# Ln and Exp ahead of the Relu check in every chunk of a gated linear attention, with a tile of its own for the Relu

## The chip, the cores and the metric

The kernel runs on one core of one Trainium2 chip. The metric is the device time of one execution in microseconds (us). A core has TensorE (PE, matrix products), VectorE (DVE), ScalarE (ACT, activation functions), GpSimd (POOL) and SyncE (SP, which issues the DMAs here). Each engine works through its own queue of instructions in order and waits at semaphores for the others. The program groups the functions of ScalarE into sets of tables, and an instruction ACT_TABLE_LOAD changes the set.

## The reference

A gated linear attention over 4 batches, 8 heads, 768 steps and a head size of 48 runs first, then a feed-forward block on its output (3072 tokens, width 384, inner width 2048):

```python
for t in range(S):
    state = alpha[:, :, t, :, None] * state + np.einsum('bhd,bhe->bhde', k[:, :, t], v[:, :, t])
    y[:, :, t] = np.einsum('bhd,bhde->bhe', q[:, :, t], state)
...
h = x @ w_in
sp = np.maximum(h, 0.0) + np.log1p(np.exp(-np.abs(h)))
g = h * erf(sp)
return (g @ w_out).astype(np.float32)
```

All tensors are float32.

## The kernel before

The attention is cut into 24 chunks of 64 steps (two groups of batches, 12 chunks each), each chunk holding 4 pairs of heads and 2 batches side by side as tiles of 128 x 512. The feed-forward block is cut into 12 blocks of 256 tokens, and each block into 4 groups of 512 inner channels. A feed-forward block starts when its two chunks of attention are done, so both parts run interleaved over the whole time.

In a chunk (class `Chunk`) the steps are: `la`, `lq`, `lv` load alpha, k with q, and v. `a1` (L260) makes the cumulative products of alpha in place in the tile A, on VectorE, with a floor. `a2` (L263 to L280) makes the reciprocal of A: on ScalarE a Relu with bias -AHI over A (L266), whose sum goes into `flags` and tells whether any product went above AHI; then Ln of A (L267), then Exp of its negative (L269), whose sum goes into `flags` too, and on VectorE one Newton step (`rw`, L273 and L275) and the product with k (L278). `a3` (L283) multiplies q by A. `a4` makes the scores (`pS`, L298), the update of the state T (`pu`, L307, with `kn`, the transposed k that ScalarE copies), and the masked scores `sT`. `a5` makes the attention's output `py` and splits it into a rounded part `x_hi` (L220, a copy) and the rest `x_lo` (L395, VectorE).

In a feed-forward block (class `Moe`) H is the first product (`ph`, L429, and its copy `hs`), U a Tanh on ScalarE, L1 two Ln and one Exp, L2 two VectorE passes (L458, L460), G a Gelu, Z two VectorE passes (L469, L471), O the second product (`acc`, L495) on a rounded half `gh` and a rest `gl` (L484, VectorE), and `out` the store. Steps `wi` and `wo` load the weights and split them (tiles `wst`, `wbuf`, `wi_hi`, `wo_hi` and so on).

Ln and Exp are in one set of ScalarE's tables (`LNEXP` in the code), Tanh and Gelu in another (`GELU`). The helper `act` (L210 to L214) remembers the set that it loaded last and puts an ACT_TABLE_LOAD (L213) ahead of a function of the other. Relu and Copy don't go through it:

```python
def act(table, *args, **kw):
    if loaded[0] != table:
        loaded[0] = table
        nc.scalar.preload_act_table_set(table)
    nc.scalar.activation(*args, **kw)
```

The order of all work is written out by hand in a string SCHED: each word is one step of a generator, and a generator's `yield` ends a step. So the words of `a2` take one piece of that function after another: the first word the Relu, the second the Ln, the third the Exp, and the next three one VectorE pass each. Words of other steps stand between them. Around chunk 7 and chunk 18 SCHED reads:

```
... v:H_2_0_0 a2_7 G_0_3 U_1_1 wo_13 a2_7 a2_7 a2_7 ...
... U_7_2 a5_16 H_7_3_1 a2_18 a2_17 U_6_3 H_7_3_1 a4_16 ... a2_18 a2_18 ...
```

The tile `r` comes from a pool with one buffer for each name, so the r of one chunk is the r of the next. `general` is a slow way for inputs whose flags are raised; it is compiled in but doesn't run here.

Of the kernel before, what the change touches and what calls it, by code (L numbers as in the profile page):

```python
# [10 lines left out]
F32 = mybir.dt.float32  # L11
# [5 lines left out]
AF = mybir.ActivationFunctionType  # L17
# [4 lines left out]
AHI = 1e15  # L22
# [125 lines left out]
def gla_moe(ctx: ExitStack, tc: tile.TileContext, qk, v, alpha, w_in, w_out, out):  # L148
    nc = tc.nc


    M, CPB, P, _, NP, NI, TC = qk.shape
# [17 lines left out]
    at = fast.enter_context(tc.tile_pool(name="at", bufs=1))  # L170
# [20 lines left out]
    flags = const.tile([P, NS, 2], F32, name="flags")  # L191
# [18 lines left out]
# [5 lines that stand above are left out]
# [9 lines left out]
            nc.vector.tensor_scalar(out=out, in0=in_, scalar1=scale, scalar2=None, op0=ALU.mult)  # L224

    T = at.tile([P, NI * NP * HD], F32, name="T", tag="T")
    nc.gpsimd.memset(T, 0.0)
    Tv = T.rearrange("p (i a d) -> p i a d", i=NI, a=NP)[:, :, :, :D]

# [3 lines left out]
    class Chunk:  # L233
# [29 lines left out]
        def a2(self):  # L263
            A = self.A[:, :, 1:]
            r = at.tile([P, NP * NI, TC], F32, name="r", tag="r")
            nc.scalar.activation(r, A, AF.Relu, bias=-AHI, accum_out=flags[:, self.n, 1:2])  # L266
            yield  # L267
            act(LNEXP, r, A, AF.Ln)
            yield  # L269
            act(LNEXP, r, r, AF.Exp, scale=-1.0, accum_out=flags[:, self.n, 0:1])  # L270
            yield
            w = at.tile([P, NP * NI, TC], F32, name="rw", tag="rw")
            nc.vector.tensor_tensor(out=w, in0=A, in1=r, op=ALU.mult)  # L273
            yield
            nc.vector.scalar_tensor_tensor(out=w, in0=w, scalar=2.0, in1=r, op0=ALU.subtract, op1=ALU.mult)  # L275
            yield
            kk = self.kq[:, 0].rearrange("p a i t -> p (a i) t")
            nc.vector.tensor_tensor(out=kk, in0=kk, in1=w, op=ALU.mult)  # L278
            yield
# [64 lines left out]
        def a5(self):  # L344
# [6 lines left out]
            for kt in range(KT):  # L351
                sums = []
                for w, d0 in PIECES[kt]:
                    if not self.first:
                        sums.append((w, d0, T, D, self.Q))
                    sums.append((w, d0, vx, HD, self.sT))
# [393 lines left out]
```

## Time and profile before

| what | value |
| --- | --- |
| median of 3 runs | 528.25 us (526.23 to 528.33) |
| the profiled execution | 526.75 us |
| its span in the profile | 525.0 us |
| PE busy | 499.5 us (95%) |
| DVE busy | 497.3 us (95%) |
| ACT busy | 485.1 us (92%) |
| table loads | 53 |
| granted TensorE clock, mean | 0.997 |

The span is what the profiler sees of the engines; the execution's own time is 1.75 us longer. A busy engine is one that works on an instruction. Matmuls are pipelined and their ends are modelled, so TensorE's busy time says little about its pace. Times of instructions are microseconds from the start of the span. An accumulated sum shows as a small instruction of its own, ACTIVATION_READ_ACCUMULATOR, right behind its activation. In a group the last columns are the engine's idle time directly ahead of its instructions and what ended it.

### The profile page before, as it was taken

How to read it: one execution, taken by the hardware profiler on the slowest of the kernel's cores; microseconds unless marked ns; L12 is line 12 of the kernel's file. 1: busy time of each engine (PE TensorE's matmuls, PEld its weight loads, DVE VectorE, ACT ScalarE, POOL GpSimd, SP SyncE). 2: the span in 40 equal slices, each digit the busy share in tenths (PEclk: the TensorE clock that was granted, in tenths of full speed). 3: DMA queues.
4: the chain of work that ended last, by engine and by line, in shares of the span. 5: the costliest groups of instructions: out<-in, count | busy, mean ns of one | idle time of the engine just before them, and what ended most of it. 6: DMA issues, size and time to landing. Idle time of an engine off the chain costs nothing.

```text
span 525.0 us, 16780 instructions
## 1 busy us (share of the span) xinstructions
PE 499.5 (95%) x7386; PEld 481.5 (92%) x7386; DVE 497.3 (95%) x715; ACT 485.1 (92%) x700; POOL 2.3 (0%) x14
## 2 busy tenths in 40 slices
PE   1699999999999999999999999999999999999994
PEld 1599999989999999999999999999999999999994
DVE  6999999999999999999999999999899999999993
ACT  6999999999999999989999899998898999999680
POOL 1000000000000000000000000000000000000000
PEclk9999999999999999999999999999999999999998
DMA  8976353341313203413012311123103120000001
GB/s 296 346 284 237 105 161 114 125 151 41 127 37 93 90 30 107 156 55 134 2 58 67 117 37 38 59 72 109 44 23 121 43 79 26 8 1 30 28 4 37
DMA packets 17936, 48.44 MB, mean 92 GB/s; under 512 B 1984, under 2 KB 5056, under 8 KB 17856
## 3 DMA queue, kind: packets, MB, share of 16 engines
q1 hardware_dynamic: 17856, 47.29, 26.6%
q8 instruction: 60, 0.98, 0.8%
q14 instruction: 20, 0.16, 0.1%
HBM read 42.57 MB, written 4.72 MB: 90 GB/s over the span
## 4 chain that ended last, share of the span: by engine, by line
PE 48%; ACT 25%; DVE 18%; issue 4%; DMA 3%; SPq 0%; DVEq 0%; ACTq 0%
PE acc L495 25%; PE ph L429 18%; ACT s L214 6%; ACT w L214 3%; ACT L213 3%; PE py L364 3%; ACT hs L220 3%; DVE t L458 2%; DVE gl L484 2%; ACT r L214 2%; DVE w L460 2%; DMA A<-in_alpha_dram 2%; ACT wbuf L220 2%; ACT wbuf L532 2%; DVE s L469 2%
## 5 line engine op out<-in xcount | busy, mean ns | idle before, releaser
L429 PE MATMUL ph<-x_hi,wi_hi 128*128 128x256 f32 x576 | 165.8, 288 | 1.8 <-ACT x_hi L220 1.1
L429 PE MATMUL ph<-x_lo,wi_hi 128*128 128x256 f32 x576 | 161.6, 281 | 1.1 <-issue 0.9
L429 PE MATMUL ph<-x_hi,wi_lo 128*128 128x256 f32 x576 | 161.3, 280 | 0.2 <-issue 0.2
L495 PE MATMUL acc<-wo_hi,gh 128*128 128x384 f32 x384 | 130.9, 341 | 0.0
L495 PE MATMUL acc<-wo_hi,gl 128*128 128x384 f32 x384 | 129.9, 338 | 0.8 <-DVE gl L484 0.6
L495 PE MATMUL acc<-wo_lo,gh 128*128 128x384 f32 x384 | 129.1, 336 | 0.0
L429 PEld LDWEIGHTS ph<-x_hi,wi_hi 128*128 128x128 f32 x576 | 109.0, 189 | 5.4 <-ACT hs L220 1.9
L429 PEld LDWEIGHTS ph<-x_hi,wi_lo 128*128 128x128 f32 x576 | 109.8, 191 | 1.0 <-issue 1.0
L429 PEld LDWEIGHTS ph<-x_lo,wi_hi 128*128 128x128 f32 x576 | 109.1, 189 | 0.6 <-DVE x_lo L395 0.5
L214 ACT ACTIVATE s<-s 128x1024 f32<-128x1024 f32 x96 | 100.1, 1054 | 6.2 <-DVE t L458 5.9
L495 PEld LDWEIGHTS acc<-wo_hi,gl 128*128 128x128 f32 x384 | 72.2, 188 | 2.6 <-DVE gl L484 2.4
L495 PEld LDWEIGHTS acc<-wo_hi,gh 128*128 128x128 f32 x384 | 72.2, 188 | 1.2
L495 PEld LDWEIGHTS acc<-wo_lo,gh 128*128 128x128 f32 x384 | 72.2, 188 | 0.0
L484 DVE TENSOR_TENSOR gl<-hs,gh 128x512 fp32r<-128x512 f32 x96 | 65.0, 689 | 6.5 <-ACT gh L220 1.7
L213 ACT ACT_TABLE_LOAD x52 | 66.7, 1283 | 0.9
L471 DVE SCALAR_TENSOR_TENSOR hs<-s,hs 128x1024 f32<-128x1024 f32 x48 | 58.6, 1222 | 0.7
L458 DVE TENSOR_TENSOR t<-s,w 128x1024 f32<-128x1024 f32 x48 | 58.2, 1219 | 1.0 <-ACT w L214 0.8
L469 DVE TENSOR_TENSOR s<-s,w 128x1024 f32<-128x1024 f32 x48 | 58.4, 1220 | 0.6
L460 DVE SCALAR_TENSOR_TENSOR w<-t,w 128x1024 f32<-128x1024 f32 x48 | 58.3, 1220 | 0.3
L220 ACT ACTIVATE hs<-ph 128x512 f32<-128x512 f32 x85 | 49.3, 590 | 3.3 <-PE ph L429 2.8
L214 ACT ACTIVATE w<-s 128x1024 f32<-128x1024 f32 x48 | 50.6, 1057 | 0.6
L214 ACT ACTIVATE s<-hs 128x1024 f32<-128x1024 f32 x48 | 50.4, 1058 | 0.4
(66 smaller groups left out, 719.3 us busy)
## 6 DMA issues: line engine op xcount, KB each, us to landing
kq<-in_qk_dram SPq DMA_DIRECT2D x24, 512.0 KB, 3.7
raw_v<-in_v_dram SPq DMA_DIRECT2D x24, 448.0 KB, 4.1
A<-in_alpha_dram SPq DMA_DIRECT2D x24, 260.0 KB, 3.3
wst<-in_moe_w_in_dram SPq DMA_DIRECT2D x12, 512.0 KB, 9.5
wst<-in_moe_w_out_dram SPq DMA_DIRECT2D x16, 384.0 KB, 3.5
out_dram<-o SPq DMA_DIRECT2D x24, 192.0 KB, 1.9
```

Of the source, the lines that this page charges most:

```text
L213: nc.scalar.preload_act_table_set(table)
L214: nc.scalar.activation(*args, **kw)
L220: nc.scalar.activation(out, in_, AF.Copy, scale=scale)
L364: nc.tensor.matmul(out=py[i][c0 : c0 + 32, kt, :], lhsT=left[r0 : r0 + rows, at0 : at0 + 32], rhs=right[r0 : r0 + rows, pair, i, :], start ...
L429: nc.tensor.matmul(out=o, lhsT=wt[:, kt, fs], rhs=xt[:, kt, :], start=n == 0, stop=n == 3 * KT - 1)
L458: nc.vector.tensor_tensor(out=t, in0=s, in1=w, op=ALU.mult)
L460: nc.vector.scalar_tensor_tensor(out=w, in0=t, scalar=2.0, in1=w, op0=ALU.add, op1=ALU.mult)
L469: nc.vector.tensor_tensor(out=s, in0=s, in1=w, op=ALU.mult)
L471: nc.vector.scalar_tensor_tensor(out=h, in0=s, scalar=RT2 / 2, in1=h, op0=ALU.subtract, op1=ALU.mult)
L484: nc.vector.tensor_tensor(out=gl.rearrange("p a t -> p (a t)"), in0=gg, in1=ghf.bitcast(F32), op=ALU.subtract)
L495: nc.tensor.matmul(out=self.acc[tt][:, :DM], lhsT=gt[:, u, ts], rhs=wt[:, f, :], start=f == 0 and n == 0, stop=f == NF - 1 and n == 2,)
L532: nc.scalar.activation(z, low.bitcast(U32), AF.Copy, scale=0.937 * 2.0**-29)
```

## The change

In `a2` the Ln and the Exp come first and the Relu third, in a step of its own between two `yield`s. The Relu no longer writes r but a new tile `above`, which is allocated once ahead of all chunks and which nothing reads. The three sums and flags are the same.

```diff
     T = at.tile([P, NI * NP * HD], F32, name="T", tag="T")
+    above = at.tile([P, NP * NI, TC], F32, name="above", tag="above")
     nc.gpsimd.memset(T, 0.0)
...
         def a2(self):
             A = self.A[:, :, 1:]
             r = at.tile([P, NP * NI, TC], F32, name="r", tag="r")
-            nc.scalar.activation(r, A, AF.Relu, bias=-AHI, accum_out=flags[:, self.n, 1:2])
-            yield
             act(LNEXP, r, A, AF.Ln)
             yield
             act(LNEXP, r, r, AF.Exp, scale=-1.0, accum_out=flags[:, self.n, 0:1])
+            yield
+            nc.scalar.activation(above, A, AF.Relu, bias=-AHI, accum_out=flags[:, self.n, 1:2])
             yield
```

SCHED is as before, so its first word for a chunk's `a2` is now the Ln, its second the Exp, its third the Relu. The table loads follow from that. On ScalarE, in chunk 7 (the Relu is `r,flags<-A` before and `above,flags<-A` after, Ln is `r<-A`, Exp is `r,flags<-r`; `s<-s` and `s<-hs` are the Gelu and the Tanh of the feed-forward block), before:

```order
L220 ACTIVATE hs<-ph 128x512
L266 ACTIVATE r,flags<-A 128x512
L214 ACTIVATE s<-s 128x1024
L214 ACTIVATE s<-hs 128x1024
L213 ACT_TABLE_LOAD
L214 ACTIVATE r<-A 128x512
L214 ACTIVATE r,flags<-r 128x512
L220 ACTIVATE x_hi<-py 128x3x64 x2
```

and with the change:

```order
L220 ACTIVATE hs<-ph 128x512
L213 ACT_TABLE_LOAD
L214 ACTIVATE r<-A 128x512
L213 ACT_TABLE_LOAD
L214 ACTIVATE s<-s 128x1024
L214 ACTIVATE s<-hs 128x1024
L213 ACT_TABLE_LOAD
L214 ACTIVATE r,flags<-r 128x512
L271 ACTIVATE above,flags<-A 128x512
L220 ACTIVATE x_hi<-py 128x3x64 x2
```

The Relu stood between `hs` and the Gelu with no load around it; the Ln that stands there now has one load ahead of it and one behind it, and the Exp has the load that the Ln had.

On ScalarE around chunk 18, where Tanh passes stand before and behind the Relu, before:

```order
L214 ACTIVATE s<-hs 128x1024
L266 ACTIVATE r,flags<-A 128x512
L214 ACTIVATE s<-hs 128x1024
L220 ACTIVATE kn<-pn 128x512
L220 ACTIVATE hs<-ph 128x512
L213 ACT_TABLE_LOAD
L214 ACTIVATE s<-s 128x1024 x2
L220 ACTIVATE gh<-hs 128x512
L214 ACTIVATE w<-s 128x1024
L214 ACTIVATE r<-A 128x512
L214 ACTIVATE r,flags<-r 128x512
```

and with the change:

```order
L214 ACTIVATE s<-hs 128x1024
L213 ACT_TABLE_LOAD
L214 ACTIVATE r<-A 128x512
L213 ACT_TABLE_LOAD
L214 ACTIVATE s<-hs 128x1024
L220 ACTIVATE kn<-pn 128x512
L220 ACTIVATE hs<-ph 128x512
L213 ACT_TABLE_LOAD
L214 ACTIVATE s<-s 128x1024 x2
L220 ACTIVATE gh<-hs 128x512
L214 ACTIVATE w<-s 128x1024
L214 ACTIVATE r,flags<-r 128x512
```

The Relu between the two Tanh passes became a Ln with a load ahead of it and one behind it; the Exp now stands where the Ln stood, and the Relu comes behind it.

At ScalarE's start, in chunk 0, before:

```order
L266 ACT_TABLE_LOAD
L266 ACTIVATE r,flags<-A 128x512
L213 ACT_TABLE_LOAD
L214 ACTIVATE r<-A 128x512
L214 ACTIVATE r,flags<-r 128x512
L220 ACTIVATE wbuf<-wst 128x512
```

and with the change:

```order
L213 ACT_TABLE_LOAD
L214 ACTIVATE r<-A 128x512
L214 ACTIVATE r,flags<-r 128x512
L271 ACTIVATE above,flags<-A 128x512
L220 ACTIVATE wbuf<-wst 128x512
```

The load on the Relu's own line is gone, and the one load left stands ahead of everything that waits for data.

## Rows read from the trace of the kernel before

**Rows 1.** The page's first part: busy us, share of the span, instructions.

```profile
PE 499.5 (95%) x7386; PEld 481.5 (92%) x7386; DVE 497.3 (95%) x715; ACT 485.1 (92%) x700; POOL 2.3 (0%) x14
```

**Rows 2.** Groups, shapes kept apart: busy us, mean ns; idle before, releasers.

```profile
L213 ACT ACT_TABLE_LOAD x52 | 66.7, 1283 | 0.9
...
L273 DVE TENSOR_TENSOR rw<-A,r 128x512 f32<-128x512 f32 x24 | 16.5, 687 | 1.5 <-ACT r L214 1.4
...
L266 ACT ACT_TABLE_LOAD x1 | 1.3, 1283 | 0.8 <-PEq L695 0.8
```

**Rows 3.** Stretches: length, busy us (instructions) by engine, clock, DMA share, GB/s.

```profile
115.00:170.00 55.00, 55.00 (x768) 53.56 (x770) 54.15 (x79) 54.73 (x80) 0.00 (x0) 1.00 0.26 83
...
313.30:363.00 49.70, 49.70 (x821) 48.22 (x820) 49.11 (x68) 48.57 (x66) 0.00 (x0) 1.00 0.21 63
366.00:510.00 144.00, 143.81 (x1665) 140.59 (x1666) 138.04 (x186) 130.88 (x158) 0.00 (x0) 1.00 0.12 39
```

**Rows 4.** TensorE in order of time: start, us, what, idle before and releaser.

```profile
170.80 0.39 PE L429 MATMUL ph<-x_hi,wi_hi 128*128 128x256 f32 x1 [0.21 <-ACT hs L220]
...
365.99 0.39 PE L429 MATMUL ph<-x_lo,wi_hi 128*128 128x256 f32 x1 [0.19 <-DVE x_lo L395]
```

**Rows 5.** Pieces of the chain that ended last: start, us, what.

```profile
305.22 1.28 ACT L213
...
310.12 1.28 ACT L213
...
496.92 4.25 PE ph L429 x36
```

**Rows 6.** The start in order of time, ScalarE and VectorE.

```profile
4.97 0.63 ACT L266 ACTIVATE r<-A 128x512 f32<-128x512 f32 x1 [2.88 <-DVE A L260]
...
5.71 1.28 ACT L213 ACT_TABLE_LOAD   x1
...
7.01 0.63 ACT L214 ACTIVATE r<-A 128x512 f32<-128x512 f32 x1
...
8.43 0.69 DVE L273 TENSOR_TENSOR rw<-A,r 128x512 f32<-128x512 f32 x1 [0.43 <-ACT r L214]
...
9.23 0.66 ACT L220 ACTIVATE wbuf<-wst 128x512 f32<-128x512 f32 x1 [0.84 <-DMA wst<-in_moe_w_in_dram]
```

**Rows 7.** Chunk 7 in order of time, ScalarE, and at the end VectorE.

```profile
99.92 0.62 ACT L266 ACTIVATE r<-A 128x512 f32<-128x512 f32 x1
...
101.48 1.05 ACT L214 ACTIVATE s<-hs 128x1024 f32<-128x1024 f32 x1
102.55 1.28 ACT L213 ACT_TABLE_LOAD   x1
103.84 0.63 ACT L214 ACTIVATE r<-A 128x512 f32<-128x512 f32 x1
...
105.04 0.18 ACT L214 ACTIVATION_READ_ACCUMULATOR r<-r 128x1 f32 x1
105.14 0.53 ACT L220 ACTIVATE x_hi<-py 128x192 fp32r<-128x192 f32 x2
...
105.26 0.69 DVE L273 TENSOR_TENSOR rw<-A,r 128x512 f32<-128x512 f32 x1 [0.72 <-ACT r L214]
```

**Rows 8.** ScalarE at the end of that stretch, with chunk 8's Relu and Ln.

```profile
114.95 0.55 ACT L220 ACTIVATE x_hi<-py 128x192 fp32r<-128x192 f32 x2 [0.25 <-PE py L364]
...
115.91 0.20 ACT L266 ACTIVATION_READ_ACCUMULATOR r<-A 128x1 f32 x1
116.14 0.63 ACT L214 ACTIVATE r<-A 128x512 f32<-128x512 f32 x1
```

**Rows 9.** ScalarE's gh and VectorE's two gl behind chunk 18's loads.

```profile
313.33 0.61 ACT L220 ACTIVATE gh<-hs 128x512 fp32r<-128x512 f32 x1
...
313.28 1.39 DVE L484 TENSOR_TENSOR gl<-hs,gh 128x512 fp32r<-128x512 f32 x2
```

## The prediction

> **What bounds the kernel now.** I read the busy times first, then the groups, the stretches, the waits of TensorE, the chain, and last the order of time at the places that the change moves. TensorE, VectorE and ScalarE are all busy for 92 to 95% of a span of 525.0 us [rows 1], so no engine has room to spare by its total, and the question is who waits for whom at each place. From 115 to 170 us ScalarE idles 0.27 us of 55 [rows 3]; TensorE is taken for busy all that time, but at 170.80 it stands and is released by ScalarE's hs [rows 4], which means that TensorE has no stock of work left there and ScalarE's lateness is its own. From 313.3 to 363 us VectorE idles 0.59 of 49.7 [rows 3], and at 365.99 TensorE is released by VectorE's x_lo [rows 4]. The chain passes through the table loads of 305.22 and 310.12, and up to 501 us it is on TensorE's [rows 5]. From 366 to 510 ScalarE idles 13 us [rows 3]; what is saved or spent on it there is worth little. So three stretches count: the start, ScalarE's until 170, and the handover from ScalarE to VectorE near 314.
>
> **The change, part by part.** By the order of instructions only ScalarE's queue changes; the other engines and the DMA issues keep theirs. What changes with it are the waits and the table loads.
>
> *The loads.* Now 52 + 1 loads of 1.283 us run [rows 2]. The Relu needs none of its own: in chunk 7 it stands among passes of the gelu set [rows 7], and the loader is called by `act` alone. Ln, which does need the Ln/Exp set, now takes Relu's place. The order shows four loads more and one fewer: two more in chunk 7, two more in chunk 18, and at the start the one on Relu's line goes. In chunk 6 one load comes earlier by four passes, which changes no count.
>
> What one load costs the queue: the pass before it ends at 101.48 + 1.05 = 102.53, the load starts at 102.55 and lasts 1.28, the next pass starts at 103.84; without a load neighbours overlap by about 0.1 (the accumulator read of 105.04 ends at 105.22, x_hi starts at 105.14) [rows 7]. So 1.28 + 0.02 + 0.1 = 1.40 us. The row of all 52 loads shows 0.9 us idle ahead of them in total, 0.02 each [rows 2]: nothing is emptied at length before a load. The Trainium skill ("ScalarE: Activation LUTs", section "What ACT_TABLE_LOAD costs") gives the same 1283 ns but adds a drain of about 1380 ns to every switch, 2.66 us in all; an estimate by that page would put the four loads at 10.6 us instead of 5.6. No row here shows that drain, and the sum goes by the rows.
>
> *Chunk 7.* Two loads more are 2.80; Exp no longer directly follows the Ln it depends on, which gives back 0.13 (below): x_hi starts about 2.7 later than 105.14 [rows 7]. Behind the Exp stands VectorE's rw: it already waits 0.72 us for r at 105.26 [rows 7] and will wait about 2.1 more, with every VectorE pass queued behind it. At 114.95 ScalarE waits 0.25 for TensorE's py [rows 8], which absorbs that much: 2.45 are left. Of the 0.27 idle up to 170 [rows 3] a part may go too. Bounds 2.1 and 2.7; I take **2.3**, since most of that idle is single hundredths between dependent passes. At 170.80 TensorE is waiting for ScalarE already [rows 4], so it starts 2.3 late, and from there on the chain is TensorE's own, which makes up nothing.
>
> *Chunk 18.* Again two loads, 2.8, less 0.1 since a Relu with an accumulator read leaves and a Ln without one comes: 2.7. ScalarE's gh of 313.33 ends at 313.94, and the second of VectorE's two gl there starts at 313.28 + 1.39 - 0.69 = 313.98 [rows 9]: VectorE has no margin at all. It comes 2.7 later, and VectorE then runs full up to 363 and hands over to TensorE at 365.99 [rows 3, 4]. The bounds are 2.7 and 2.1 (if all of the 0.59 idle were made up); I take **2.6**, nearer the upper end because VectorE sits on the chain itself.
>
> *The start.* Today: Relu at 4.97, a load at 5.71, Ln at 7.01 [rows 6]. With the load of Relu's line gone, `act` loads its own set while ScalarE waits for the scan anyway, and Ln starts at 4.97: 2.04 earlier. But VectorE idles only 0.43 for r before rw at 8.43 [rows 6]: it is busy with three scans and a product until then. And ScalarE's next pass waits until 9.23 for the DMA of wst [rows 6], which the change doesn't touch, and VectorE needs what comes of it. Bounds 0 and 0.43; I take **0.2 gained**.
>
> *The waits.* Relu and Ln write the same r, so Ln waits for Relu's end: from the accumulator read to Ln 0.23 us (115.91 to 116.14) [rows 8], where an independent pass follows it in 0.10 (105.04 to 105.14) [rows 7]. That is 0.13. The order has Relu directly ahead of Ln in 14 chunks and Ln directly ahead of Exp in 14; afterwards only Ln ahead of Exp remains, in 15, while the new third pass writes a tile that nobody waits for. So 13 of these gaps go, 1.7 us of ScalarE. Worth something only where ScalarE sets the pace: chunks 5, 8 and 10 before 170 us, 3 x 0.13 = **0.4 gained** (chunk 1 is in the start's term, chunk 7 counted above). The bounds are 0 and 1.7.
>
> *Costed at nothing.* r comes one pass earlier in every chunk, but VectorE's rw waits for r 1.4 us in all and three times only [rows 2], at 8.43 and 105.26 above all, both counted. The later Relu delays nobody: its flags are read at the end, and A is read later still by the next chunk. The wait on VectorE for the old r moves from Relu to Ln, in the same place of the queue. In chunk 6 the earlier load makes wo_hi, x_hi and gh up to 1.4 late, but what stands behind them is on time again; the cover is that VectorE has other passes ready, and if it had none, up to 1.4 would be added. The tile `above` takes 2 KB of each partition and moves the buffers allocated behind it; no row shows a dependence on addresses.
>
> **The sum.** 2.3 + 2.6 - 0.2 - 0.4 = +4.3 us. The profiled execution took 526.75 us: 531.05. The median of the three runs, 528.25, is 1.5 above that execution, and would give 532.55; the runs shown scatter over 2.1, so I forecast the middle, **531.8 us**. From no change a measurement here can tell about 0.5%, 2.6 us.
>
> **The rivals.**
> *One pair is absorbed.* If TensorE or VectorE has inputs in stock that the view of busy times hides, one delay of 2.3 to 2.6 vanishes and +1.7 to +2.0 is left, 528.5 to 530.2. Against it: both waits of TensorE [rows 4] are exactly behind these places. For it: they are short, 0.2 us, and 60 and 50 us downstream. Chance 0.20.
>
> *Not slower: the shorter chain of r wins.* The mechanism is the start and the dropped waits, with the loads hidden. If VectorE's order had room there, the whole 2.04 at the start [rows 6] and 13 x 0.13 would come through, 3.7 us; with both pairs hidden that is 523.1 to 524.6. If only the terms I took come through, -0.6, 526.2 to 527.7. It decides at TensorE's waits of 170.80 and 365.99: were its stock there over 2.7 us, the loads would be free. The full VectorE from 9 us on and the DMA at 9.23 speak against the gain, the waits against the hiding. Chance 0.16, a quarter of it for over 0.5% faster, the rest within.
>
> *Dearer loads.* Chunk 6's moved load bites as well, 1.4, and nothing is absorbed: 2.7 + 2.7 + 1.4 = +6.8, 533.6 to 535.1. The Trainium skill's drain (same page and section), 2.66 for each switch, would end near 536.8, an estimate by that page; the 0.02 ahead of each load [rows 2] leaves it almost nothing. Chance 0.06 for both.
>
> **How the numbers follow.** The forecast has 0.58. Slower by over 0.5% means above 530.9: nearly all of the forecast (0.54), the dearer loads (0.06) and a quarter of the absorbed pair (0.05), together 0.65. Within 0.5%: the rest of the absorbed pair (0.15) and of the third case (0.12), 0.27. Faster: 0.08, the quarter of 0.16 and another 0.04 of the forecast's for scatter. The range goes from 527.5, which takes in the absorbed pair and the start of the not-slower case, to 535.0, the dearer loads by rows.
>
> **What would show it.** Right: 56 loads; rw in chunk 7 waiting over 2 us for r; VectorE waiting over 2 us for gh after 313; TensorE standing 2 us longer in all before 171, and again before 370; no gap between the accumulator read and Relu. Wrong: those waits without a longer span, or a first TensorE pass over 1 us earlier, or loads with idle time of a microsecond ahead of them.

## The result and the profile after

The changed kernel takes **534.38 us** (median of 4 runs, 533.90 to 535.24), the kernel before 527.46 us beside it (4 runs, 526.23 to 528.33). The ratio is 1.0135 with a 95% interval of 1.0106 to 1.0164: slower by 6.9 us, where the sum had 4.3. The direction and the range of the prediction hold; a term of the sum is too small. Two single runs of later kernels, some 170 us above the others of their kernel at a mean granted clock of 0.67, are left out of every time below. The mean granted clock of the changed kernel's four runs was 0.991, 0.998, 0.990 and 0.999; the two at 0.99 took 535.24 and 534.70 us, the other two 534.05 and 533.90. The profiled execution is the one of 535.24 us, with a span of 533.5. It is the longest of the four, and the profiled one of the kernel before, 526.75, lies under its median, so the two traces differ by 8.5 us and not by 6.9. In the changed file the lines behind L227 stand one further down; the helper stays at L213 and L214.

The page's busy times, and from its groups the table loads and one group of VectorE (busy us, mean ns; idle just ahead, and what ended most of it):

```profile
PE 503.3 (94%) x7386; PEld 484.0 (91%) x7386; DVE 497.4 (93%) x715; ACT 488.2 (91%) x703; POOL 2.4 (0%) x14
...
L213 ACT ACT_TABLE_LOAD x56 | 71.8, 1283 | 1.8 <-PEq L696 0.8
...
L485 DVE TENSOR_TENSOR gl<-hs,gh 128x512 fp32r<-128x512 f32 x96 | 64.9, 687 | 10.0 <-ACT gh L220 4.7
```

Beside [rows 1, 2]: three loads more of the same 1283 ns each, and VectorE's work is the same to 0.1 us. So for VectorE the 8.5 us that the span is longer are time in which it stands. The next rows show where it starts. ScalarE in chunk 7, in order of time (start, duration, what):

```profile
100.60 1.28 ACT L213 ACT_TABLE_LOAD   x1
101.89 0.63 ACT L214 ACTIVATE r<-A 128x512 f32<-128x512 f32 x1
102.54 1.28 ACT L213 ACT_TABLE_LOAD   x1
103.84 1.06 ACT L214 ACTIVATE s<-s 128x1024 f32<-128x1024 f32 x1
...
105.86 1.28 ACT L213 ACT_TABLE_LOAD   x1
107.16 0.63 ACT L214 ACTIVATE r<-r 128x512 f32<-128x512 f32 x1
107.70 0.18 ACT L214 ACTIVATION_READ_ACCUMULATOR r<-r 128x1 f32 x1
107.79 0.61 ACT L271 ACTIVATE above<-A 128x512 f32<-128x512 f32 x1
108.40 0.53 ACT L220 ACTIVATE x_hi<-py 128x192 fp32r<-128x192 f32 x2
```

Against [rows 7], one load has become three; x_hi starts at 108.40 and not at 105.14. Relu follows the accumulator read without a gap (107.70 to 107.79). VectorE behind it, in chunk 6, in chunk 7, at the next update of the state T, and behind chunk 18 (idle ahead and releaser in brackets):

```profile
78.96 0.56 DVE L555 TENSOR_TENSOR wo_lo<-wbuf,wo_hi 128x384 fp32r<-128x384 f32 x1 [0.58 <-ACT wo_hi L220]
...
107.92 0.69 DVE L274 TENSOR_TENSOR rw<-A,r 128x512 f32<-128x512 f32 x1 [2.82 <-ACT r L214]
...
114.29 0.62 DVE L324 TENSOR_TENSOR T<-T,pu 128x192 f32<-128x192 f32 x2 [0.56 <-PE pu L308]
...
321.23 0.69 DVE L485 TENSOR_TENSOR gl<-hs,gh 128x512 fp32r<-128x512 f32 x1 [2.67 <-ACT gh L220]
```

The rw wait of [rows 7] grew from 0.72 to 2.82 us; the second gl of [rows 9], which stood right behind the first, now waits 2.67; and wo_lo waits 0.58 where it waited for nothing. Set beside the same instructions before, VectorE is 0.8 us late from 78 us, 2.7 at rw, 5.0 at 116 us, 4.5 at 279, 7.3 at 315, 8.1 at 370 and 8.4 at the end. TensorE's largest waits at those places, in order of time:

```profile
111.43 0.58 PE L299 MATMUL pS<-kq 48*64 48x64 f32 x5 [2.18 <-DVE kq L279]
...
316.92 0.33 PE L308 MATMUL pu<-raw_v,kn 64*64 64x48 f32 x8 [1.28 <-ACT kn L220]
...
331.89 0.39 PE L430 MATMUL ph<-x_hi,wi_hi 128*128 128x256 f32 x1 [0.93 <-ACT hs L220]
```

It stands 2.2 us behind each pair of loads, but at 111 and at 317 to 332 us, not as late as 171 and 366 [rows 4]. At the handover behind chunk 18 its wait stayed as it was, 0.20 us:

```profile
373.25 0.39 PE L430 MATMUL ph<-x_lo,wi_hi 128*128 128x256 f32 x1 [0.20 <-DVE x_lo L396]
```

A stand without a releaser that the kernel before had near chunk 7 shrank to 0.20 at 108.39. The row before:

```profile
108.51 0.28 PE L429 MATMUL ph<-x_lo,wi_hi 128*128 128x256 f32 x1 [0.88 <-issue]
```

After the first of its new stands TensorE's clock falls. The stretches around it (length, busy us of PE, PEld, DVE, ACT, POOL, granted clock, DMA share, GB/s), before and then after:

```profile
112.00:116.00 4.00, 4.00 (x145) 3.71 (x144) 4.00 (x8) 3.72 (x8) 0.00 (x0) 1.00 0.53 145
116.00:120.00 4.00, 4.00 (x33) 4.00 (x33) 3.72 (x7) 3.94 (x11) 0.00 (x0) 1.00 0.35 134
```

```profile
108.00:112.00 4.00, 1.62 (x22) 1.22 (x21) 3.86 (x8) 4.00 (x11) 0.00 (x0) 0.93 0.08 13
112.00:116.00 4.00, 4.00 (x66) 3.91 (x59) 3.41 (x6) 4.00 (x8) 0.00 (x0) 0.50 0.40 117
116.00:120.00 4.00, 4.00 (x139) 3.74 (x138) 3.10 (x5) 1.93 (x2) 0.00 (x0) 0.72 0.57 192
```

From 112 to 116 us the granted clock is 0.50, which is the lower of TensorE's two levels, 1.2 instead of 2.4 GHz; before, it was 1.00 throughout there. A stretch with a mean of 0.72 has the lower level for 2 x 0.28 of its time; over the three stretches that makes 0.6 + 4.0 + 2.2 = 6.8 us. TensorE counts as busy, yet ScalarE is busy for 1.93 of the last 4 us: its x_hi at 120.25 waits for TensorE's py. The same instruction, at 114.95 before, waited 0.25 [rows 8].

```profile
120.25 0.55 ACT L220 ACTIVATE x_hi<-py 128x192 fp32r<-128x192 f32 x2 [2.28 <-PE py L365]
```

So ScalarE's lateness came back to it by way of VectorE and a TensorE at half clock. After chunk 18's stand the clock stays at 1.00.

At the start nothing was gained. ScalarE's rows there, then TensorE's:

```profile
4.90 0.63 ACT L214 ACTIVATE r<-A 128x512 f32<-128x512 f32 x1 [2.80 <-DVE A L261]
...
9.60 0.67 ACT L220 ACTIVATE wbuf<-wst 128x512 f32<-128x512 f32 x1 [2.65 <-DMA wst<-in_moe_w_in_dram]
```

```profile
10.55 1.76 PE L299 MATMUL pS<-kq 48*64 48x64 f32 x28 [10.55 <-DVE kq L279]
```

Ln runs at 4.90 instead of 7.01 [rows 6], as the term said, but wst's copy starts at 9.60 instead of 9.23, waiting 2.65 us for the DMA, and TensorE's first matmul is at 10.55, where it was at 10.62.

### The profile page after: what moved, and what is told of

Its sections match the earlier page's. It is cut to its first block, busy times and chain, and to the rows that moved or that the text cites. A ratio compares the mean times of both kernels' runs of the same rounds, so it can differ in the third digit from the quotient of the medians.

```text
span 533.5 us, 16784 instructions
## 1 busy us (share of the span) xinstructions
PE 503.3 (94%) x7386; PEld 484.0 (91%) x7386; DVE 497.4 (93%) x715; ACT 488.2 (91%) x703; POOL 2.4 (0%) x14
## 4 chain that ended last, share of the span: by engine, by line
DVE 41%; PE 33%; ACT 19%; issue 4%; DMA 1%; SPq 0%; DVEq 0%; ACTq 0%
PE acc L496 17%; PE ph L430 12%; DVE t L459 6%; DVE w L461 5%; DVE gl L485 5%; DVE hs L472 4%; ACT s L214 4%; DVE s L470 4%; ACT L213 3%; ACT r L214 2%; ACT wbuf L533 2%; DVE A L261 2%; ACT hs L220 2%; DVE sT L329 2%; ACT wbuf L220 2%
## 5 line engine op out<-in xcount | busy, mean ns | idle before, releaser
L214 ACT ACTIVATE s<-s 128x1024 f32<-128x1024 f32 x96 | 100.1, 1055 | 7.0 <-DVE t L459 6.6
L213 ACT ACT_TABLE_LOAD x56 | 71.8, 1283 | 1.8 <-PEq L696 0.8
L214 ACT ACTIVATE w<-s 128x1024 f32<-128x1024 f32 x48 | 50.7, 1058 | 0.6
L299 PE MATMUL pS<-kq 48*64 48x64 f32 x768 | 38.7, 235 | 13.2 <-DVE kq L279 13.0
```

The costliest lines, as they stand in the source:

```text
L299: nc.tensor.matmul(out=ps[half * HD : (half + 1) * HD, pair * NI + i, :], lhsT=K[rows, pair, i, :], rhs=Q[rows, pair, i, :], start=True, s ...
```

## The experiments

Each kernel was timed beside the kernel before, whose median was 527.5 to 527.6 us each time. In these kernels lines stand a few further down than in the kernel before (rw, for one, at L278 instead of L273). "Old order" means Relu, Ln, Exp, "new order" Ln, Exp, Relu.

### Are the loads at these places the whole loss?

The changed kernel with the old order in chunks 6, 7 and 18 alone (the Relu still writes `above`):

```diff
+            if self.n in (6, 7, 18):
+                nc.scalar.activation(above, A, AF.Relu, bias=-AHI, accum_out=flags[:, self.n, 1:2])
+                yield
             act(LNEXP, r, A, AF.Ln)
             yield
             act(LNEXP, r, r, AF.Exp, scale=-1.0, accum_out=flags[:, self.n, 0:1])
             yield
-            nc.scalar.activation(above, A, AF.Relu, bias=-AHI, accum_out=flags[:, self.n, 1:2])
-            yield
+            if self.n not in (6, 7, 18):
+                nc.scalar.activation(above, A, AF.Relu, bias=-AHI, accum_out=flags[:, self.n, 1:2])
+                yield
```

> The changed kernel with Relu ahead again in chunks 6, 7 and 18 alone (52 loads instead of 56). If the loads at these places are the whole loss, it is back at the kernel before or up to 1 us under it: 526.5 to 527.5 us. If the new order in the other 21 chunks, or the place of the new tile in memory, costs time by itself, it stays at 529 us or above.

Measured: 527.55 us, ratio 1.0007 (0.9992 to 1.0021). The loss sits in those three chunks, to within about 1 us (the interval is -0.4 to +1.1). The new order in the other 21 chunks, chunk 0 among them, and the new tile are worth nothing that can be measured, in either direction. This left chunk 6 as a suspect beside 7 and 18, so each was then done alone.

### One chunk at a time

The kernel before with the new order in one chunk (7, then 18, then 6), the Relu writing `above` there:

```diff
-            nc.scalar.activation(r, A, AF.Relu, bias=-AHI, accum_out=flags[:, self.n, 1:2])
-            yield
+            if self.n != 7:
+                nc.scalar.activation(r, A, AF.Relu, bias=-AHI, accum_out=flags[:, self.n, 1:2])
+                yield
...
+            if self.n == 7:
+                nc.scalar.activation(above, A, AF.Relu, bias=-AHI, accum_out=flags[:, self.n, 1:2])
+                yield
```

> The kernel before with the new order in chunk 7 alone (55 loads). Theory of the delay alone: VectorE's rw comes 2.1 us late, nothing else follows, 529.5 to 530. Theory that TensorE's standing costs more than the delay (a second wait at pu, a halved clock in part of the runs): 530.5 to 531.5, runs with a lower granted clock about 1 us above the others. Rival, that part is absorbed until 170 us: under 529.

> The kernel before with the new order in chunk 18 alone (55 loads). The delay at VectorE's gl passes in full: plus 2.6 to 2.8, 530.1 us. Rival, that VectorE's and TensorE's stock downstream absorbs part: 528 to 529.

> The kernel before with the new order in chunk 6 alone: as many loads as before (53), one of them four passes earlier. The prediction costed this at nothing: 527.5 us, as before. If VectorE's wo_lo waiting about 0.6 us for wo_hi, as in the changed kernel's trace at 79 us, passes to the end: plus 0.5 to 0.8, 528.2 us. If all of the load's 1.4 us passes: 528.9.

Measured: chunk 7 alone 530.87 us, ratio 1.0065 (1.0050 to 1.0080), **+3.3 us**; chunk 18 alone 530.04, 1.0047 (1.0034 to 1.0060), **+2.5**; chunk 6 alone 528.15, 1.0013 (1.0004 to 1.0022), **+0.7**. Together 6.5, of the 6.9 measured. VectorE's rw and TensorE's pS with the new order in chunk 7 alone:

```profile
107.45 0.69 DVE L278 TENSOR_TENSOR rw<-A,r 128x512 f32<-128x512 f32 x1 [2.81 <-ACT r L214]
```

```profile
110.96 0.39 PE L303 MATMUL pS<-kq 48*64 48x64 f32 x6 [2.55 <-DVE kq L283]
```

and the stretches there, columns as above:

```profile
108.00:112.00 4.00, 1.45 (x48) 1.25 (x48) 3.86 (x8) 4.00 (x10) 0.00 (x0) 0.98 0.18 36
112.00:116.00 4.00, 4.00 (x40) 3.91 (x38) 3.97 (x8) 4.00 (x8) 0.00 (x0) 0.59 0.54 180
```

The stand and the fall of the clock come with chunk 7 alone (here 3.4 us at the lower level); VectorE's lag is 2.2 us at rw, 3.0 at 116 us and 3.3 from 118 us on. With the new order in chunk 18 alone the clock's mean stays between 0.997 and 0.999, and VectorE's gl waits for gh:

```profile
315.72 0.69 DVE L489 TENSOR_TENSOR gl<-hs,gh 128x512 fp32r<-128x512 f32 x1 [2.74 <-ACT gh L220]
```

There the price, 2.5, is no more than the delay of two loads. In chunk 6 the one moved load makes wo_lo wait 0.58 us, as in the changed kernel, which is close to the 0.7 that it costs.

### What of chunk 7's price is ScalarE's, and what TensorE's?

The same as chunk 7 alone, but in the hand-written order the word of the Exp stands right behind that of the Ln, ahead of the Gelu and the Tanh. The loads are as many, but VectorE gets r earlier:

```diff
-... v:H_2_0_0 a2_7 G_0_3 U_1_1 wo_13 a2_7 a2_7 a2_7 H_2_0_1
+... v:H_2_0_0 a2_7 a2_7 G_0_3 U_1_1 wo_13 a2_7 a2_7 H_2_0_1
```

> The kernel with the new order in chunk 7 alone, and chunk 7's second word moved up to the first, so that Ln and Exp follow each other ahead of the Gelu and the Tanh: again two loads more than before (55), but only two ahead of x_hi instead of three, and r ready about 3 us earlier, so that VectorE and TensorE don't stand at one place. If the price in chunk 7 is ScalarE's time, 2.7 us wherever the loads stand: 530.3 to 530.9. If it is the standing of VectorE and TensorE at rw and pS, with the half clock behind it: 528 to 529.5, and the granted clock stays at 0.996 or above.

Measured: 529.71 us, 1.0046 (1.0031 to 1.0061), **+2.1**, between the two expectations; its seven runs (528.99 to 530.42) all lie below the six of chunk 7 alone (530.47 to 531.88). The clock's mean was 0.996 to 0.999 in all runs, and rw waits for nothing. But the loads' lateness now reaches VectorE at x_lo, and TensorE's stand at pS is half as long, with two more behind it:

```profile
107.41 0.36 DVE L400 TENSOR_TENSOR x_lo<-py,x_hi 128x192 fp32r<-128x192 f32 x1 [1.76 <-ACT x_hi L220]
```

```profile
110.10 0.39 PE L303 MATMUL pS<-kq 48*64 48x64 f32 x6 [1.26 <-DVE kq L283]
...
118.56 0.39 PE L434 MATMUL ph<-x_hi,wi_hi 128*128 128x256 f32 x1 [0.45 <-ACT x_hi L220]
...
123.01 0.39 PE L434 MATMUL ph<-x_hi,wi_hi 128*128 128x256 f32 x1 [0.69 <-ACT hs L220]
```

```profile
112.00:116.00 4.00, 4.00 (x145) 3.70 (x144) 3.96 (x9) 4.00 (x8) 0.00 (x0) 1.00 0.39 119
```

About 2.1 of chunk 7's 3.3 us come with ScalarE's two loads wherever r stands, and some 1.2 more where VectorE and TensorE wait in the middle. TensorE's three stands here make 2.40 us, hardly less than the 2.55 of its one stand there, so how long it stands in sum is not the difference; that its clock falls after the one long stand, and not after these, is one.

A second try: TensorE was given work to fill its stand, half of one feed-forward product H, done twice (18 matmuls ahead of the waiting pS; the second pass writes the same values, so the output is unchanged). Once on chunk 7 alone, once on the changed kernel:

```diff
-                for kt in range(KT):
+                for _ in range(2 if (self.n, g, half) == (2, 1, 1) else 1):
+                    n = 0
+                    for kt in range(KT):
...
```

> The kernel with the new order in chunk 7 alone, and one half H of block 2, which stands directly ahead of the place where TensorE waits 2.55 us, computed twice into the same PSUM tile (18 more matmuls, about 2.1 us by the 0.118 us each of the trace), so that TensorE works in that gap. Theory that the clock falls because TensorE stands, and that this costs 0.7 to 1.2 of the 3.3 us: the granted clock stays at 0.996 or above and the time is 529.7 to 530.2. Rival, that the clock has no part in the loss: 530.8 as without the filling, or above, since 2.1 us of work are added.

> The changed kernel with the same half H computed twice. Theory of the clock: no half clock at 112 to 118 us, and the time falls by about 1 us from 534.4 to 533.2 to 533.6 although TensorE does 2.1 us more. Rival: 534.4 or above.

Measured: 534.36 us, 1.0133 (1.0118 to 1.0148), and 536.04, 1.0168 (1.0148 to 1.0188). As totals both fall to their rivals ("or above"), that the clock has no part in the loss. But the totals cannot decide it, as the traces show. Locally the first did what it was meant to do (its profiled run, 537.18, is the longest of five); TensorE's wait and the stretch that had been at 0.59:

```profile
111.60 0.38 PE L303 MATMUL pS<-kq 48*64 48x64 f32 x5 [0.43 <-DVE kq L283]
```

```profile
112.00:116.00 4.00, 4.00 (x91) 3.74 (x91) 3.97 (x9) 4.00 (x7) 0.00 (x0) 1.00 0.67 211
```

With the clock at 1.00, VectorE's lag grows by 2.3 us across chunk 7 (0.74 to 3.08) and no further until 210 us; without the added work it grew by 3.2 (0.10 to 3.29). But then stands appear that have no releaser, and with them new stretches at a lower clock (the same kernel, first TensorE, then a stretch):

```profile
207.17 0.57 PE L303 MATMUL pS<-kq 48*64 48x64 f32 x13 [1.20 <-issue]
...
291.65 0.28 PE L436 MATMUL ph<-x_hi,wi_hi 128*128 128x256 f32 x1 [2.51 <-issue]
```

```profile
208.00:212.00 4.00, 4.00 (x23) 4.00 (x22) 3.91 (x6) 3.59 (x5) 0.00 (x0) 0.58 0.10 33
```

On the changed kernel the same happens: the stretch that had been at 0.50 is back at full clock,

```profile
112.00:116.00 4.00, 4.00 (x98) 3.74 (x96) 3.97 (x8) 4.00 (x8) 0.00 (x0) 1.00 0.54 191
```

but there is a stand of 0.79 at 205.66 and one of 2.00 at 289.70, both "issue", and a mean clock of 0.70 from 208 to 212. The kernel before has such stands too, of 0.88 at 108.51 and 0.23 at 204.29. So the totals say nothing on the clock at chunk 7.

The five traces can be set side by side. The table has TensorE's stands between 104 and 125 us in sum, the time at the lower clock there, and by how much VectorE's mean lateness against the kernel before grew between the stretch of 95 to 104 us and that of 119 to 170 us (by the kernel before's times), all in us:

| kernel | TensorE stands | at the lower clock | VectorE's lateness grew by |
| --- | --- | --- | --- |
| new order in 7, Exp early | 2.4 | 0 | 2.5 |
| new order in 7, H twice | 0.7 | 0 | 2.3 |
| changed, H twice | 0.8 | 0 | 2.2 |
| new order in 7 | 2.6 | 3.4 | 3.2 |
| changed | 2.4 | 6.8 | 4.7 |

The last column goes with the time at the lower clock and not with the time that TensorE stands. The six kernels without more loads in chunk 7 have -0.4 to +0.2 there; that is its scatter. The runs point the same way, with less: of the six of chunk 7 alone, the one with a mean clock of 0.998 took 530.47 us, 0.5 under the median of the others. So the lower clock is a part of chunk 7's price. With one trace of each kernel its size stays open: 0.5 by the runs, 0.7 to 1.0 by the traces, at most the 1.2 above.

### Is a load dear by itself?

The kernel before with one load ahead of chunk 21's Relu and one behind it, at 376 us, where ScalarE has idle time soon after:

```diff
+            if self.n == 21:
+                nc.scalar.preload_act_table_set(GELU)
             nc.scalar.activation(r, A, AF.Relu, bias=-AHI, accum_out=flags[:, self.n, 1:2])
+            if self.n == 21:
+                nc.scalar.preload_act_table_set(LNEXP)
             yield
```

> The kernel before, order untouched, with two loads more in chunk 21, one on each side of its Relu (to the gelu set and back), at 375 us, where the chain is on TensorE and ScalarE idles 13 of the 144 us that follow 366. If a load costs only where ScalarE is waited for: 527.5 to 528.3. If two loads cost 2.5 us or more wherever they stand: 530 or above.

Measured: 527.80 us, 1.0001 (0.9989 to 1.0014): nothing. The two loads and the first pass behind them that still waits:

```profile
376.27 1.28 ACT L267 ACT_TABLE_LOAD   x1
...
378.31 1.28 ACT L270 ACT_TABLE_LOAD   x1
...
395.81 1.06 ACT L214 ACTIVATE s<-s 128x1024 f32<-128x1024 f32 x1 [1.33 <-DVE t L462]
```

In the kernel before ScalarE had these waits:

```profile
380.56 0.63 ACT L220 ACTIVATE gh<-hs 128x512 fp32r<-128x512 f32 x1 [1.45 <-PE acc L495]
...
394.73 1.06 ACT L214 ACTIVATE s<-s 128x1024 f32<-128x1024 f32 x1 [2.05 <-DVE t L458]
```

The first of them is gone and the second is shorter: the loads went into idle time.

### The waits on r, and the version without the extra loads

The kernel before with the Relu writing `above` in its old place, so that Ln no longer waits for it:

```diff
-            nc.scalar.activation(r, A, AF.Relu, bias=-AHI, accum_out=flags[:, self.n, 1:2])
+            nc.scalar.activation(above, A, AF.Relu, bias=-AHI, accum_out=flags[:, self.n, 1:2])
             yield
```

> The kernel before, order untouched, with the Relu writing the new tile, so that Ln no longer waits for it. The prediction's term for the waits gives minus 0.4 us, at most minus 1.7: 526 to 527.2. If the gaps are made up by other waits at once, 527.5, no change. If the tile's place in memory costs, above 528.5.

Measured: 527.23 us, 0.9996 (0.9986 to 1.0007). Chunk 8's rows show that the gap closed:

```profile
115.88 0.20 ACT L268 ACTIVATION_READ_ACCUMULATOR above<-A 128x1 f32 x1
115.97 0.63 ACT L214 ACTIVATE r<-A 128x512 f32<-128x512 f32 x1
```

0.09 us from the read to Ln, where it was 0.23 [rows 8]. The total of -0.25 us cannot be told from nothing.

Last, the changed kernel with words of chunks 6, 7 and 18 moved in the hand-written order, so that Ln again stands where it stood and the loads are 52, as here for chunk 7:

```diff
-... v:H_2_0_0 a2_7 G_0_3 U_1_1 wo_13 a2_7 a2_7 a2_7 H_2_0_1
+... v:H_2_0_0 G_0_3 U_1_1 wo_13 a2_7 a2_7 a2_7 a2_7 H_2_0_1
```

> The changed kernel with the first word of chunks 6, 7 and 18 moved in the hand-written order to just ahead of the second, so that Ln stands behind the passes of the other set (52 loads). If only the loads cost, 526 to 527.5 us, at or a little under the kernel before, since r in chunk 7 comes 0.6 us earlier than there. If the order Ln, Exp, Relu costs by itself, above 528.5.

Measured: 528.72 us, 1.0019 (1.0005 to 1.0033). Most of the loss is undone, but about 1 us stays, just inside what was named for the order costing by itself. The run with the old order in the three chunks, whose other 21 have the new order, speaks against that. At the start wst's copy is at 9.93 here, 0.70 later than before [rows 6], and VectorE is 0.8 us late by 74 us, ahead of the first moved word, as it is at the end; whether that is the whole of it was not tried. No version tried is faster than the kernel before by more than its interval.

## Why the prediction was right, and what it mis-sized

- **The mechanism was right.** Loads of 1.283 us, put where ScalarE is waited for, make the loss: the old order in three chunks takes it back, and the same loads at 376 us cost nothing. Most marks came as named: 56 loads, rw waiting 2.82 us, gl waiting 2.67, no gap ahead of the Relu. TensorE stood 2.2 us longer from 300 to 375 us, but from 104 to 180 only 1.4 longer in all, since the stand of 0.88 shrank.
- **Chunk 18's term was right:** 2.6 predicted, 2.5 measured alone. VectorE carried 2.7 from gl to 360 us, as said. TensorE's part was another: it stood at 317 and 332 us, because kn and hs came late, and not at the handover, where its wait is 0.20 after and 0.19 before.
- **Chunk 7's term was too small,** and this is the step that failed: "Bounds 2.1 and 2.7; I take **2.3**", against 3.3 measured alone. (Its lower bound, 2.45 less 0.27, comes to 2.2.) ScalarE's own delay was as said: x_hi starts at 107.94 with chunk 7 alone, 2.8 us later. The term named VectorE's later rw too, but priced ScalarE's lateness only, to TensorE's wait at 170.80 [rows 4], and took the 0.25 us at 114.95 [rows 8] as room. In fact VectorE's wait at rw passes to TensorE's pS 3.5 us later. TensorE stands there for over 2 us, then runs at the lower clock, and the x_hi of 114.95 waits for it not 0.25 us but 2.28 in the changed kernel (0.73 with chunk 7 alone). Where the clock stays at full level VectorE's lateness grows by 2.2 to 2.5, about what the term had, and chunk 7 with r earlier costs 2.1 in the runs; so the fall of the clock is the likeliest part that the term lacked. What it costs is known only as 0.5 to 1.2. The runs of the changed kernel at a mean clock of 0.99 were 1.0 us longer than those at 0.998 and 0.999, which fits.
- **Chunk 6's load was costed at nothing, with 1.4 as its bound; it cost 0.7.** The cover named was that VectorE has other passes ready. VectorE takes its passes in order, and wo_lo was the next: it waited 0.58 us.
- **The start's 0.2 did not come.** Ln came 2.1 us earlier, but the copy of wst waited for its DMA, VectorE's product of q and A ahead of rw did too (0.62 us, where it waited for nothing), and the first matmul moved by 0.07 us only. It was in the term's bounds (0 to 0.43).
- **The waits' 0.4 cannot be told.** With them alone removed the kernel came out at -0.25 us, inside its interval of nothing. The gaps close as said.
- **The sum** so becomes 3.3 + 2.5 + 0.7 = 6.5 us, of 6.9 measured, and both gains fall away. That the range still held is in part luck: its upper end was the case of dearer loads, which had a chance of 0.06, and 534.38 is 2.6 us above the forecast of 531.8 and 0.6 under that end.
- **The rivals.** No pair was absorbed and the shorter chain of r did not win. "Dearer loads" gave the time best (+6.8), but in part for another reason: chunk 6's load did bite, while 2.7 for chunk 7 is still short of 3.3, and chunk 18 stayed below it. A drain ahead of each load is not there: a load starts 0.02 us behind the pass before it (101.89 + 0.63 = 102.52, load at 102.54), and two loads cost 2.5 us in chunk 18. The Trainium skill ("ScalarE: Activation LUTs", section "What ACT_TABLE_LOAD costs") counts some 1380 ns of drain to every switch. Here the measurement speaks against it, while its 1283 ns for the load itself agrees.

## What to carry to other kernels

A pass that needs no load between passes of either set, as the Relu here, can be moved without one; a Ln put in its place between two passes of the other set brings two (chunks 7 and 18), so look at what each slot of the order runs between, not at the number of passes. Price a delay by following every waiter behind it, VectorE and TensorE too, to where it returns: counted on ScalarE alone, chunk 7 came out 1 us too cheap. Where nothing waits, the same loads cost nothing.

## What the runs showed of the hardware that was not expected

TensorE's granted clock fell to half after stands of 2.2 and 2.6 us at pS near 111 us; it did not fall after stands of 1.28 and 0.93 us at 317 and 332 us. The length of the stand alone does not decide it: with H done twice it fell (a mean of 0.58 from 208 to 212) after stands of 0.32 and 1.20 us near 207, and stayed at 1.00 around the stand of 2.51 us at 291 us.

Stands without any releaser ("issue") move and grow when instructions are added to TensorE's queue: with 18 matmuls and their weight loads more than chunk 7 alone, one of 1.20 us appeared at 207 us, and one of 2.51 at 291.65 where there had been one of 0.35 at 288.94; the kernel took 3.5 us longer. The packets of DMA queue q8, which the page lists as "instruction" (60 of 16 KB), tell more. In the twelve traces there are 20 such stands of 0.2 us and over, and each ends 2.2 to 2.8 us after one of these packets started (packet at 106.24 and end at 108.51 in the kernel before, 204.36 and 207.17 with H twice on chunk 7 alone). These stretches of 0.6 us behind 60 packets are only some 7% of the 525 us. So TensorE seems to wait there for its own instructions to arrive; no run was made to show it.
